# Gated mix of softmax attention and a linear-attention branch: a build-time list scheduler orders all engines, and branch B is rewritten token-major

## The chip, the cores and the metric

One core of one Trainium2 chip. The metric is the device time of one execution in microseconds (us), lower is better. Executions of one kernel usually agree within about 1%; a run more than 1.5% above the fastest of the same kernel is called slow and is left out of ratios. Engines: PE is TensorE (matmuls), PEld its weight loads, DVE is VectorE, ACT is ScalarE, POOL is GpSimd, SP issues DMAs.

## The reference, cut to what matters

2048 tokens, width 512, 32 heads of 16. Inputs and output are bf16.

```python
g = sigmoid((x * gate_w).sum(-1))                     # one gate per token
a = softmax(q k^T / 4) v  @ A_wo                      # branch A: 32 full 2048 x 2048 attentions
pq, pk = q' w_phi, k' w_phi                           # branch B: its own q', k', v'
phi_q = [softmax(pq), softmax(-pq)]; phi_k likewise   # 32 features per head
b = (phi_q (phi_k^T v')) / (phi_q sum(phi_k) + 1e-6)  @ B_wo
out = g * a + (1 - g) * b
```

Branch A needs 32 x 2048 x 2048 exponentials. They are the largest single piece of work, and in both kernels only ACT makes them.

## The kernel before

Scores of branch A are made transposed, as "units" of 128 keys x 512 queries of one head, four heads (a "pack") side by side on 32 rows each of the PE array. Five PSUM banks form a ring; ACT takes three units, then two, then three. The scores of group k need the banks that group k-2 has left, so PE can be two groups ahead of ACT and no more.

```python
def _emit_st_group(self, k):                 # scores ("QK")
    for u in range(ua, ub + 1):
        if k >= 2: deps.append((self.c_exp.sem, k - 1))        # exponential k-2 is done
        self.op("pe", lambda e: e.matmul(self.ps_ring[:, u % 5, :],
            self.kT_d[32*i:32*i+32, ...], self.qT_ring[32*i:32*i+32, ...], tile_position=(32*i, 0)), ...)
def _emit_exp_op(self, k):                   # 819 of them, 128 x 1536 or 128 x 1024
    self.op("act", lambda e: e.activation(self.ET[...], self.ps_ring[...], ACT.Exp, scale=0.25), ...)
# _emit_pv_pack: ps_ot[32*i:32*i+17] += Vaug . ET; the 17th column of V is ones, for the denominator
```

Everything else, the "side work", is put into slots between the packs by hand-made rules. It shares two PSUM banks (`mp`), and a projection is one block of four 256-column matmuls:

```python
for p in range(NPACK):
    self._run_conts(p)                       # readers put off, parts 2 and 3 of a feature tile
    for k in ops_first_at_pack[p]: self._emit_st_group(k)
    if p >= LAG: self._emit_pv_pack(p - LAG)
    for k in ops_at_pack[p]: self._emit_exp_op(k)
    self._run_side(p)                        # projections, branch B, outputs
def _proj_block(...):
    for c in range(4):
        self.op("pe", lambda e: e.matmul(mp[:, 0:256], lhs_fn(c), rhs_fn(c), start=(c == 0), stop=(c == 3)), ...)
    # then a DVE copy, put off by one slot
```

Branch B projects q' and k', multiplies by w_phi, subtracts maximum and minimum on DVE, takes 128 exponentials of 128 x 256, normalises, and works in two halves of the heads. All of x and of the weights is loaded before the first projection. Outputs for three quarters of the tokens are made at the very end, 128 columns at a time.

The softmax here doesn't subtract the row's maximum and nothing guards it: scores larger than these inputs give would overflow.

## Time and profile before

Median 1185.89 us of 4 runs (1182.9 to 1190.98). The profiled execution takes 1185.6 us. I split it by ACT: before the first score exponential starts (head), from there to the end of the last one (middle), and after it (tail).

| us | kernel before |
|---|---|
| head | 27.1 |
| middle: ACT busy | 989.7 |
| middle: ACT idle | 151.9 |
| tail | 16.9 |

From the page of the kernel before: the span, the busy times, the clock that PE was granted in 40 slices (tenths of full), and the largest group of instructions (busy us, mean ns of one, then idle before them and who ended it).

```profile
span 1185.6 us, 14920 instructions
PE 937.5 (79%) x5848; PEld 277.9 (23%) x5856; DVE 553.6 (47%) x1424; ACT 990.9 (84%) x949; POOL 22.4 (2%) x28
...
PEclk9965555667577566655575757757567556565567
...
L504 ACT ACTIVATE ET<-ps_ring 128x1536 bf16<-128x1536 f32 (+1 forms) x819 | 952.6, 1252 | 172.5 <-PE ps_ring L449 168.6
```

ACT bounds the kernel, and it waits for scores. The clock is between half and three quarters nearly everywhere. Three lines of the waits view (total us, times, longest), the first for ACT, the others for PE itself:

```profile
ACT ET L504 <- PE ps_ring L449: 168.6, 155, 25.1
...
PE ps_ot L474 <- DVE T_63 L512: 21.1, 15, 3.1
...
PE ps_mp L778 <- DVE kvz_acc L791: 9.4, 10, 1.5
```

The last two: PE stands at a matmul whose input, or whose bank, DVE has not finished. Adding up all idle time of PE in the middle that DVE ended gives 74.2 us (53.1 in front of side work, 21.1 in front of PV).

The timeline, here around a k projection:

```profile
119.05 1.04 PE L621 MATMUL ps_mp<-xT,WA 128*128 128x256 bf16 x4
120.02 0.12 PEld L449 LDWEIGHTS ps_ring<-qT_ring,kT_d 32*128 32x128 bf16 x5 [0.41 <-ACT ET L504]
120.02 1.03 PE L449 MATMUL ps_ring<-qT_ring,kT_d 32*128 32x512 bf16 x5
...
120.73 5.97 ACT L504 ACTIVATE ET<-ps_ring 128x1536 bf16<-128x1536 f32 x5 [0.87 <-PE ps_ring L449]
```

The exponential waited 0.87 us for scores that stood behind the projection in PE's queue. The end of the kernel is worse; this is the output projection at 128 columns, two banks and a DVE instruction between:

```profile
1151.11 0.66 PE L911 MATMUL ps_mp<-WoA_d,onT_A 128*128 128x128 bf16 x8 [0.22 <-DVE outt L916]
1151.54 0.61 DVE L916 SCALAR_TENSOR_TENSOR outt<-ps_mp,gcol,outB 128x128 bf16<-128x128 f32 x2 [0.23 <-PE ps_mp L911]
1152.34 0.61 PE L911 MATMUL ps_mp<-WoA_d,onT_A 128*128 128x128 bf16 x8 [0.57 <-DMA out_dram<-outt]
...
1155.35 1.02 ACT L504 ACTIVATE ET<-ps_ring 128x1024 bf16<-128x1024 f32 x1 [3.12 <-PE ps_ring L449]
```

### The profile page before, as it was taken

What the parts mean: (1) busy time and instruction counts of PE and PEld (TensorE: products, weight loads), DVE (VectorE), ACT (ScalarE), POOL (GpSimd) and SP (SyncE); (2) the same over time, 40 slices, a digit from 0 to 9 for tenths busy, and PEclk for the clock granted to TensorE, in tenths of its full rate; (3) what the DMA queues carried; (4) which work ended last, traced back from release to release, by engine and by line L of the source; (5) the groups of instructions that cost most, each with busy time, mean ns of one, the idle gap of its engine ahead of it and who ended that gap; (6) DMA issues with size and microseconds to landing.
All of it is one profiled execution on the core that took longest, in us unless ns stands there. A gap on an engine that the chain in (4) does not pass through costs nothing.

```text
span 1185.6 us, 14920 instructions
## 1 busy us (share of the span) xinstructions
PE 937.5 (79%) x5848; PEld 277.9 (23%) x5856; DVE 553.6 (47%) x1424; ACT 990.9 (84%) x949; POOL 22.4 (2%) x28
## 2 busy tenths in 40 slices
PE   4978888888778878888877877877878687787784
PEld 2422212222222222222121222212222112222132
DVE  4411111153663664645455255455563656446435
ACT  1898898989899998988898989988898788688651
POOL 4000000000000000000000000000000000000011
PEclk9965555667577566655575757757567556565567
DMA  5100000100000000000000000000000000000001
GB/s 124 37 1 1 1 1 1 54 1 2 1 1 1 1 1 1 1 1 1 1 1 1 1 1 1 1 1 1 1 1 1 1 1 1 1 2 1 0 32 41
DMA packets 13110, 9.36 MB, mean 8 GB/s; under 512 B 10736, under 2 KB 11760, under 8 KB 13040
## 3 DMA queue, kind: packets, MB, share of 16 engines
q1 hardware_dynamic: 12000, 4.74, 1.7%
q0 software_dynamic: 1040, 3.67, 0.9%
q8 instruction: 46, 0.75, 0.3%
q14 instruction: 24, 0.20, 0.1%
HBM read 4.21 MB, written 2.10 MB: 5 GB/s over the span
## 4 chain that ended last, share of the span: by engine, by line
PE 42%; ACT 29%; DVE 16%; issue 9%; another core or an unknown queue 1%; DMA 1%; SPq 1%; DVEq 0%; ACTq 0%; POOL 0%
ACT ET L504 28%; PE ps_ring L449 16%; PE ps_ot L474 11%; PE ps_mp L621 9%; DVE T_63 L512 2%; PE ps_mp L880 2%; DVE bmx L727 1%; DVE bsub L729 1%; DVE brc L748 1%; DVE bsub L732 1%; DVE bmx L725 1%; DVE brc L745 1%; ACT bexp L739 1%; SPq L540 1%
## 5 line engine op out<-in xcount | busy, mean ns | idle before, releaser
L504 ACT ACTIVATE ET<-ps_ring 128x1536 bf16<-128x1536 f32 (+1 forms) x819 | 952.6, 1252 | 172.5 <-PE ps_ring L449 168.6
L449 PE MATMUL ps_ring<-qT_ring,kT_d 32*128 32x512 bf16 x2048 | 427.0, 542 | 137.7 <-ACT ET L504 130.9
L474 PE MATMUL ps_ot<-ET,Vaug 128*17 128x512 bf16 x2048 | 281.5, 539 | 21.4 <-DVE T_63 L512 21.1
L449 PEld LDWEIGHTS ps_ring<-qT_ring,kT_d 32*128 32x128 bf16 x2048 | 78.8, 97 | 384.6 <-ACT ET L504 306.4
L474 PEld LDWEIGHTS ps_ot<-ET,Vaug 128*17 128x17 bf16 x2048 | 50.7, 90 | 246.9 <-issue 209.2
L689 DVE CAST qkT_B<-ps_mp 128x256 bf16<-128x256 f32 x64 | 27.1, 423 | 94.0 <-PE ps_mp L621 94.0
L653 DVE CAST kT_d<-ps_mp 128x256 bf16<-128x256 f32 x32 | 13.6, 425 | 97.8 <-PE ps_mp L621 97.7
L621 PE MATMUL ps_mp<-xT,WqT_v 128*128 128x256 bf16 x256 | 56.9, 367 | 1.8 <-DVE kvz_acc L791 1.4
L621 PE MATMUL ps_mp<-xT,WB 128*128 128x256 bf16 x256 | 54.4, 354 | 0.0
L670 DVE CAST qT_ring<-ps_mp 128x256 bf16<-128x256 f32 x64 | 26.9, 420 | 46.7 <-PE ps_mp L621 46.5
L512 DVE STREAM_TRANSPOSE T_63<-ps_ot 128x512 f32<-128x512 f32 x32 | 22.8, 714 | 47.3 <-PE ps_ot L474 47.0
L512 DVE STREAM_TRANSPOSE T_63<-ps_mp 128x512 f32<-128x512 f32 x32 | 22.9, 717 | 42.1 <-remote 29.9
L621 PE MATMUL ps_mp<-xT,WA 128*128 128x256 bf16 x128 | 28.7, 382 | 17.1 <-DMA xT<-in_A_x_dram 16.9
L725 DVE TENSOR_REDUCE bmx<-ps_mp 128x16 f32<-128x256 f32 x64 | 26.9, 420 | 28.4 <-PE ps_mp L718 28.4
L888 DVE CAST outB<-ps_mp 128x256 bf16<-128x256 f32 x32 | 13.6, 425 | 53.0 <-PE ps_mp L880 53.0
L944 PE MATMUL ps_mp<-WoA_d,onT_A 128*128 128x128 bf16 x64 | 17.0, 291 | 25.7 <-DVE oacc L955 6.6
L880 PE MATMUL ps_mp<-WoB_d,onT_Bc 128*128 128x256 bf16 x128 | 36.1, 381 | 0.2 <-DVE qT_ring L670 0.2
L892 DVE TENSOR_TENSOR outB<-ps_mp,outB 128x256 bf16<-128x256 f32 x32 | 13.6, 425 | 45.3 <-PE ps_mp L880 45.3
L745 DVE TENSOR_REDUCE brc<-bexp 128x16 f32<-128x256 bf16 x64 | 26.6, 416 | 15.5 <-ACT bexp L739 14.4
L621 PEld LDWEIGHTS ps_mp<-xT,WqT_v 128*128 128x128 bf16 x256 | 25.7, 120 | 29.7 <-PE ps_ring L449 10.7
L621 PEld LDWEIGHTS ps_mp<-xT,WB 128*128 128x128 bf16 x256 | 25.2, 118 | 25.7 <-issue 18.0
L812 PE MATMUL ps_mp<-iden,phiq_tile 128*128 128x128 bf16 x128 | 19.1, 303 | 14.9 <-DVE phi_qTc L821 8.4
(73 smaller groups left out, 662.9 us busy)
## 6 DMA issues: line engine op xcount, KB each, us to landing
out_dram<-outt POOLq DMA_DIRECT2D x16, 128.0 KB, 2.0
WA<-in_A_wqkv_dram POOLq DMA_DIRECT2D x1, 1536.0 KB, 8.2
WB<-in_B_wqkv_dram SPq DMA_DIRECT2D x1, 1536.0 KB, 7.6
wphi<-in_B_w_phi_dram SPq DMA_DIRECT2D x32, 0.5 KB, 1.6
WoA_d<-in_A_wo_dram SPq DMA_DIRECT2D x1, 512.0 KB, 4.5
WoB_d<-in_B_wo_dram SPq DMA_DIRECT2D x32, 16.0 KB, 1.6
xT<-in_A_x_dram SPq DMA_TRANSPOSE x4, 5.8
gw<-in_gate_w_dram SPq DMA_DIRECT2D x4, 0.2 KB, 2.5
```

Of the source, the lines that this page charges most:

```text
L449: tgt = self.op("pe", lambda e, b=b, g=g, kt=kt, ri=ri, i=i: e.matmul(self.ps_ring[:, b, :], self.kT_d[32 * i:32 * i + 32, g // 2, kt * TO ...
L474: last = self.op("pe", lambda e, i=i, h=h, kt=kt, sl=sl: e.matmul(self.ps_ot[32 * i:32 * i + VSL, :], self.Vaug[:, kt, h, :], self.ET[:, s ...
L504: tgt = self.op("act", lambda e, b0=b0, b1=b1, s0=s0, s1=s1: e.activation(self.ET[:, s0:s1 + 1, :], self.ps_ring[:, b0:b1 + 1, :], ACT.Exp ...
L512: d1 = self.op("dve", lambda e: e.transpose(self.T1[:].rearrange("p b s -> p (b s)"), src_bank_ap), deps=deps, counter=self.c_dve)
L621: last = self.op("pe", lambda e, c=c, mp=mp: e.matmul(mp[:, 0:out_cols], lhs_fn(c), rhs_fn(c), start=(c == 0), stop=(c == 3)), deps=(list( ...
L670: evac_fn=lambda e, mp: e.tensor_copy(self.qT_ring[:, ri, 256 * hc:256 * hc + 256], mp[:, 0:256]),
L689: evac_fn=lambda e, mp: e.tensor_copy(self.qkT_B[:, s, cl, 256 * hc:256 * hc + 256], mp[:, 0:256]),
L725: r1 = self.op("dve", lambda e: e.tensor_reduce(self.bmx[:, 0, :], pb3, AX.X, ALU.max), deps=[last, prev_exp], counter=self.c_dve)
L745: q1 = self.op("dve", lambda e: e.tensor_reduce(self.brc[:, 0:16], bexp0.rearrange("p (h f) -> p h f", f=DH), AX.X, ALU.add), deps=[a1, B. ...
L812: last = self.op("pe", lambda e, gg=gg, mpb=mpb, src=src: e.transpose(mpb[:, P * gg:P * gg + P], src[:, P * gg:P * gg + P], self.iden[:, : ...
L880: last = self.op("pe", lambda e, pr=pr, P4=P4, mp=mp: e.matmul(mp[:, 0:256], self.onT_Bc[:, ob, pr, tt * TOK:(tt + 1) * TOK], self.WoB_d[: ...
L944: m = self.op("pe", lambda e, mp=mp: e.matmul(mp[:, 0:128], self.onT_A[:, qc, pr, tt * TOK:(tt + 1) * TOK], self.WoA_d[:, pr, cols], start ...
```

## The change

The intent: let a scheduler at build time place every instruction of every engine, so that ACT never waits; start ACT earlier; and make branch B cheaper. The scheduler simulates the five engines with assumed durations. Each instruction has a priority and an earliest time; score groups always go first. It also hands out the two PSUM banks. Its result is a fixed order for each engine with semaphore waits. (A "head group" below is four heads with one quarter of the queries; there are 32.) Cut to its core:

```diff
+class Sched:
+    LAT = 0.09                                   # assumed time for a semaphore, us
+    def run(self):
+        ...                                      # pick the engine that can start first, and on it
+                                                 # the ready instruction of highest priority;
+                                                 # take a free bank, or wait until one is freed
+o_qk = s.op("pe", 0.42, [qk(x) for x in range(ua, ub + 1)], deps, prio=-1e5 + k)
+s.op("act", w * 0.427 + 0.09, ... ACT.Exp, ..., prio=tu)
+self.o_pv[p] = s.op("pe", 0.40, [pv(p, i) for i in range(4)], deps, prio=...)
+def c_mm(n): return max(0.075, n * 0.75e-3)      # assumed for a side matmul of n columns
+def proj(self, lhs, rhs, n, ...):                # four matmuls, each placed by itself
+    for c in range(4):
+        m = s.op("pe", self.c_mm(n), lambda e, c=c: e.matmul(self.bk(b)[:, 0:n], lhs(c), rhs(c),
+            start=(c == 0), stop=(c == 3)), ...)
-    self._run_side(p)                            # the hand-made slots go
```

The rest of it, abridged line by line. "Token-major" in the title means that branch B is now normalised with the tokens, not the features, on the 128 partitions:

```diff
+self.d_x.append(dma("sp", [xpart(j, c) for c in range(4)], ...))       # x in quarters, weights in slices
-rhs_fn=lambda c: self.xT[:, c, c0:c0 + 256], out_cols=256             # projections 512 columns wide
+rhs = self.xT[:, c, qc * QCH:(qc + 1) * QCH]
-lhs_fn=lambda c: self.WqT_v[:, c, g, :]                               # q projected twice, zero padded
+self.qT = bank * self.par[:, par]                                     # once, masked at the evacuation
-matmul(..., self.qkT_B[...], self.wphi[...])                          # q' then times w_phi, minus max, min
+self.Wp = WB^T . blockdiag(w_phi)                                     # composed once; features = x . Wp
+activation(self.phi[...], bank(128 x 512), ACT.Exp, scale=+1 or -1)   # 64, straight from PSUM
-self._norm_chain(mp, self.T2B, ...)                                   # DVE transposes for B
+transposes on PE; den * (1 + 1e-6 term) * exp(gate) folded in         # (1-g)/g, so one factor g at the end
+s.op("pe", self.c_mm(512), ... WoB x4, WoA x4 into one bank)          # outputs 512 wide, spread out
```

One slip in the new kernel: the gate's matmuls look up their bank through a variable that later code rebinds. In the order as shipped it happens to be the right bank.

## The prediction

> **What bounds the kernel now.** ScalarE's exponentials, but it is kept waiting. The page gives ACT 990.9 us busy of 1185.6; the groups give 952.6 us of that to the 819 score exponentials. By the windows its idle time is: 27 us before the first exponential; about 8 us in 27:100, 16 in 100:250, 12 in 250:400, 38 in 400:800, 27 in 800:1000, 30 in 1000:1137, 21 in 1137:1169 (the output projections queue on two PSUM banks and on the output DMA); 17 us after the last one. The table of waits names one cause: the exponential waits for the score matmuls, 155 times, 168.6 us (one of them the 25 us start). In the timeline each such wait follows a block of four 256-column projection matmuls put in front of the scores: 1.0 us at the low clock, costing 0.5 to 0.9 us.
>
> **What changes.**
> 1. Exponential work on ACT: scores unchanged. Feature exponentials go from 128 of 256 elements (427 ns) to 64 of 512. The Trainium skill, "ScalarE: Activation LUTs", section "What ACT_TABLE_LOAD costs", gives 186 ns + 0.833 ns per element with about 93 ns overlap; the trace agrees (1465 ns for 1536, 1038 for 1024). So an estimate of 0.52 us each, 33 us; ACT total about 985 us, hardly less than now.
> 2. Head: x arrives in quarters and only one slice of the weights is needed. Now four transposing DMAs issue for 13.4 us and PE starts at 16.9; a quarter should be there at about 7, first exponential at 12 to 14 (gain 14 us).
> 3. Tail: the last tiles keep only one block out of eight; 17 us becomes about 10 (gain 7). The output jam before it goes (gain about 20).
> 4. PE: padded q projections halve (65.5k to 32.8k columns), the q,k-times-Phi step goes; side columns 352k to 308k, in units of one 512-column matmul between score groups, not four.
> 5. DVE: 554 us falls to an estimated 275 to 300 (no max/min/subtract, no B norm chain). Off the critical path; it only frees banks sooner.
>
> **What limits it then.** Floor: 13 + 985 + 10 = about 1008 us. But PE is nearly as full. The trace's clock is 0.5 or 1.0, nothing between (mean 0.632), as the skill's "TensorE: Matmul & The Clock Gate", Part 1, says. At 0.5 a group of score matmuls, a PV pack, and each change of matmul kind start 0.54 us apart (0.43 without a change). Per 5 units ACT needs 2.40 us (985/410); PE at the low clock needs an estimated 2 x 0.54 + 1.25 x 0.54 + about 0.8 for side work = 2.5 to 2.6 us, at the high clock about 1.6. So ACT waits in low-clock stretches and hardly in high ones; I estimate 35 us of middle idle, against 152 now.
>
> **Predicted: 1042 us**, 8 in 10 between 1012 and 1085. Faster by over 2%: 0.97; within 2%: 0.02; slower: 0.01.
>
> **What would show it.** First score exponential at 12 to 14 us; ACT busy 980 to 990 us, 93 to 96% of the span; waits of the exponential on score matmuls 45 to 60 us in all, short ones (under 0.5 us); DVE under 310 us; mean clock 0.55 to 0.7; last exponential about 10 us before the end; no stretch like 1137:1169.
>
> **What would make it wrong.** The evenly spread side work keeps the clock at 0.5 throughout: then PE bounds, 1070 to 1090 us. Or the build-time durations (0.42 us per score group, 0.75 ns a column) differ from the chip's so that the fixed order makes ACT wait for feature projections. Or the clock stays high: near 1010.

## More of the kernel before

Section 4 of the page follows the chain of work that ended last, from the end of the kernel back to its start:

```profile
PE 42%; ACT 29%; DVE 16%; issue 9%; another core or an unknown queue 1%; DMA 1%; SPq 1%; DVEq 0%; ACTq 0%; POOL 0%
```

DVE's own work stands on that chain for 16% of the span. ("issue" is time in which an engine waited for nothing that the profile shows.) Its direct part in ACT's waits is smaller. After the start, ACT waits 154 times for scores, 143.5 us. For each of these waits I take what PE did from the end of the exponential that frees the banks to the first score matmul, and share the wait out in proportion (an estimate from the trace): about 82 us go to side matmuls that PE was executing, 31 to PE standing for DVE, 20 to PV, and 10 to the rest. How much of the 82 came late because of an earlier stall, this count does not tell.

## The result, and the profile after

Median 1072.49 us of 4 runs (1065.91 to 1084.18, one of them slow), against 1185.89. The ratio of the fast runs is 0.9014 (95% interval 0.8961 to 0.9066). Such a ratio, here and below, is the mean time of one kernel's fast runs over that of the kernel before in the same rounds, so it is not quite the ratio of the medians. The profiled execution took 1064.1 us.

| us | before | after | difference |
|---|---|---|---|
| head | 27.1 | 12.8 | -14.3 |
| middle: ACT busy | 989.7 | 976.0 | -13.7 |
| middle: ACT idle | 151.9 | 65.6 | -86.3 |
| tail | 16.9 | 9.7 | -7.2 |
| span | 1185.6 | 1064.1 | -121.5 |

The page of the new kernel, the same lines:

```profile
span 1064.1 us, 11915 instructions
PE 923.9 (87%) x5216; PEld 213.4 (20%) x5216; DVE 276.2 (26%) x478; ACT 977.3 (92%) x886; POOL 3.0 (0%) x8
...
PEclk9998966956566655555555565655556855555565
...
L511 ACT ACTIVATE ET<-ps_ring 128x1536 bf16<-128x1536 f32 (+1 forms) x819 | 948.2, 1294 | 72.6 <-PE ps_ring L497 57.9
...
L651 ACT ACTIVATE phi<-ps_mp 128x512 bf16<-128x512 f32 x64 | 35.5, 622 | 1.1 <-PE ps_mp L419 0.7
```

PE is busy for nearly as long as before, at the same mean clock (0.626, before 0.632). What has shrunk is DVE's work, to half, and the waits. The waits view of the new kernel:

```profile
ACT ET L511 <- PE ps_ring L497: 57.9, 112, 9.2
...
ACT ET L511 <- PE ps_ot L529: 11.6, 9, 3.5
...
PE ps_mp L670 <- DVE phi L657: 3.2, 7, 1.0
...
PE ps_ot L529 <- DVE T_73 L541: 1.7, 5, 0.6
```

The longest of the 112 waits, 9.2 us, is the start; in the middle 48.7 us are left. The second line is a wait that the prediction did not have: for PV, which frees the exponentials' output slots. All idle time of PE that DVE ended is now 10.7 us in the middle (9.0 and 1.7), where it was 74.2. DVE's share of the chain in section 4 of the page falls from 16% to 4%:

```profile
ACT 49%; PE 46%; DVE 4%; issue 1%; DMA 0%; SPq 0%
```

The tail, from the timeline: the last exponentials run through, and only one block per token tile is left after them.

```profile
1039.35 15.11 ACT L511 ACTIVATE ET<-ps_ring 128x1536 bf16<-128x1536 f32 x13
...
1056.66 0.71 DVE L553 STREAM_TRANSPOSE onT_A<-T_75 128x512 bf16<-128x512 bf16 x1
1057.43 1.04 PE L725 MATMUL ps_mp<-WoA,onT_A 128*128 128x512 bf16 x2 [2.32 <-DVE onT_A L553]
```

What is left of ACT's idle time depends on the clock, which in the trace is either 1.0 or 0.5:

| between first and last score exponential | us at clock 1.0 | ACT idle in them | us at clock 0.5 | ACT idle in them |
|---|---|---|---|---|
| before | 281.8 | 22.3 (7.9%) | 859.8 | 129.6 (15.1%) |
| after | 254.8 | 5.8 (2.3%) | 786.8 | 59.8 (7.6%) |

Two theories had to be tested. One about the gain: where did the 86 us of idle time go? My own answer was finer interleaving (single matmuls between score groups); rivals are less and longer work, and an order that knows when DVE will be done. One about the rest: are the remaining 66 us due to the low clock, or to too much PE work, or to wrongly assumed durations?

### The profile page after: what moved, and what is told of

Read it like the earlier page. It is cut to its first block, busy times and chain, and to the rows that moved or that the text cites. A ratio compares the mean times of both kernels' runs of the same rounds, so it can differ in the third digit from the quotient of the medians.

```text
span 1064.1 us, 11915 instructions
## 1 busy us (share of the span) xinstructions
PE 923.9 (87%) x5216; PEld 213.4 (20%) x5216; DVE 276.2 (26%) x478; ACT 977.3 (92%) x886; POOL 3.0 (0%) x8
## 4 chain that ended last, share of the span: by engine, by line
ACT 49%; PE 46%; DVE 4%; issue 1%; DMA 0%; SPq 0%
ACT ET L511 48%; PE ps_ring L497 18%; PE ps_ot L529 10%; PE ps_mp L419 8%; PE ps_mp L725 5%; PE ps_mp L670 2%; ACT phi L651 2%; PE ps_mp L682 1%; PE ps_mp L702 1%; DVE phi L657 1%; DVE fsum L655 1%; PE ps_mp L617 0%; DVE T_73 L541 0%; SPq L365 0%; DVE frec L656 0%
## 5 line engine op out<-in xcount | busy, mean ns | idle before, releaser
L511 ACT ACTIVATE ET<-ps_ring 128x1536 bf16<-128x1536 f32 (+1 forms) x819 | 948.2, 1294 | 72.6 <-PE ps_ring L497 57.9
L497 PE MATMUL ps_ring<-qT,kT 32*128 32x512 bf16 x2048 | 447.5, 543 | 113.1 <-ACT ET L511 108.9
L497 PEld LDWEIGHTS ps_ring<-qT,kT 32*128 32x128 bf16 x2048 | 82.9, 97 | 447.8 <-ACT ET L511 358.6
L655 DVE TENSOR_REDUCE fsum<-phi 128x64 f32<-128x1024 bf16 x32 | 39.0, 1218 | 266.6 <-ACT phi L651 266.6
L419 PE MATMUL ps_mp<-Wp,xT 128*128 128x512 bf16 x128 | 64.7, 577 | 0.0
L419 PE MATMUL ps_mp<-xT,WA 128*128 128x512 bf16 x128 | 51.2, 477 | 8.1 <-DMA xT<-in_A_x_dram 7.6
L657 DVE TENSOR_TENSOR phi<-phi,frec 128x1024 bf16<-128x1024 bf16 x32 | 39.1, 1222 | 0.8
L651 ACT ACTIVATE phi<-ps_mp 128x512 bf16<-128x512 f32 x64 | 35.5, 622 | 1.1 <-PE ps_mp L419 0.7
L725 PE MATMUL ps_mp<-WoA,onT_A 128*128 128x512 bf16 x64 | 32.2, 574 | 4.5 <-DVE onT_A L553 3.0
L725 PE MATMUL ps_mp<-WoB,onT_B 128*128 128x512 bf16 x64 | 33.6, 599 | 0.0
L419 PE MATMUL ps_mp<-WBV,xT 128*128 128x512 bf16 x64 | 25.1, 507 | 0.3 <-ACT phi L651 0.3
L670 PE MATMUL ps_mp<-iden,phi 128*128 128x128 bf16 x128 | 20.7, 299 | 3.2 <-DVE phi L657 3.2
L454 DVE CAST Vaug<-ps_mp 128x128 bf16<-128x128 f32 (+1 forms) x32 | 13.4, 425 | 30.6 <-PE ps_mp L419 30.4
```

The costliest lines, as they stand in the source:

```text
L419: m = s.op("pe", self.c_mm(n), lambda e, c=c: e.matmul(self.bk(b)[:, 0:n], lhs(c), rhs(c), start=(c == 0), stop=(c == 3)), deps if c == 0 ...
L497: return lambda e: e.matmul(self.ps_ring[:, x % RING, :], self.kT[32 * i:32 * i + 32, g // 2, kt * P:(kt + 1) * P], self.qT[32 * i:32 * i ...
L511: self.o_exp.append(s.op("act", w * 0.427 + 0.09, lambda e, b0=b0, s0=s0, w=w: e.activation(self.ET[:, s0:s0 + w, :], self.ps_ring[:, b0:b ...
L651: ex.append(s.op("act", 0.53, lambda e, sg=sg: e.activation(self.phi[:, ph.idx, :, sg, :], self.bk(b).rearrange("p (h f) -> p h f", f=DH), ...
L655: rd = s.op("dve", 1.15, lambda e: e.tensor_reduce(self.fsum[:, fs.idx, :], flat(), AX.X, ALU.add), ex, r + 10)
L657: sc = s.op("dve", 1.15, lambda e: e.tensor_tensor(flat(), flat(), self.frec[:, fs.idx, :, None].to_broadcast([P, 64, DH]), ALU.mult), [rc ...
```

## The experiments

Twelve variants ran, all with correct results. Ratios are against the kernel before in the same rounds; the new kernel has 0.9014.

| run | median us | ratio | mean clock, profiled | ACT idle in the middle, us |
|---|---|---|---|---|
| after | 1072.49 | 0.9014 | 0.626 | 65.6 |
| e9_blind | 1145.31 | 0.9629 | 0.569 (slow) | 163.8 (slow) |
| e2_block | 1051.07 | 0.8847 | 0.663 | 57.3 |
| e13_narrow | 1066.22 | 0.8971 | 0.614 | 68.2 |
| e12_q_twice | 1065.10 | 0.8962 | 0.663 | 66.1 |
| e4_wait_all | 1080.51 | 0.9092 | 0.628 | 65.9 |
| e8_late_out | 1058.07 | 0.8889 | 0.635 | 50.3 |
| e3_recal | 1069.36 | 0.9005 | 0.584 | 72.7 |
| e5_warmdur | 1060.29 | 0.8934 | 0.645 | 60.5 |
| e1_double | 1075.35 | 0.9066 | 0.725 | 82.8 |
| e6_ring512 | 1061.54 | 0.8922 | 0.878 (slow) | 74.3 (slow) |
| e7_adapt | 1024.22 | 0.8545 | 0.963 | 20.4 |
| e11_before_heat | 1276.81 | 1.0734 | 0.773 | 223.3 |

Where the profiled execution was a slow run it says so; totals and ratios use the fast runs. The "slow" runs here are single executions of one core, more than 1.5% above that kernel's fastest.

### Where the gain came from

**e2_block**: the four matmuls of a projection as one unit again.

```diff
-        for c in range(4):
-            m = s.op("pe", self.c_mm(n), lambda e, c=c: e.matmul(...), ...)
+        m = s.op("pe", 4 * self.c_mm(n), [lambda e, c=c: e.matmul(...) for c in range(4)], deps, ...)
```

> The four matmuls of a projection are one unit again, as in the kernel before; everything else as in the new one. If it is the single matmuls between score groups that gave the gain in the middle: waits of about 0.7 us at about 96 projections, 40 to 80 us more, 1105 to 1150. If the gain came from the smaller amount of PE and DVE work alone: no change, 1060 to 1080.

Measured: 1051 us, 2% *less* than the new kernel (0.8847, interval 0.8810 to 0.8884). So my theory falls: in the new order it is not the single matmuls that give the gain. A block still makes a score group late at the low clock, as this timeline of e2_block shows:

```profile
601.81 1.89 PE L417 MATMUL ps_mp<-xT,WA 128*128 128x512 bf16 x4
...
603.63 0.86 PE L495 MATMUL ps_ring<-qT,kT 32*128 32x512 bf16 x5
...
604.29 4.62 ACT L509 ACTIVATE ET<-ps_ring 128x1536 bf16<-128x1536 f32 x4 [1.07 <-PE ps_ring L495]
...
605.79 0.39 PE L495 MATMUL ps_ring<-qT,kT 32*128 32x512 bf16 x3 [0.76 <-ACT ET L509]
```

But it holds up no more than the same work in pieces: the idle share of ACT at the low clock is 7.6% in both kernels. And soon after this block, at 605.79 us, a group of score matmuls takes 0.39 us where one takes 0.61 at the low clock: the clock has gone up, a point that comes back below.

**e13_narrow** and **e12_q_twice**: undo "longer" and "less".

```diff
 # e13_narrow
+        for lo in range(0, n, 256):          # two times four matmuls of 256 columns
 # e12_q_twice
+        for par in range(2):
+            b, m = self.proj(...)            # the q projection made again for the second head
```

> The 512-column projections as two times four matmuls of 256 columns, one evacuation as in the new kernel: the same columns, 448 more matmuls. Rival F (longer matmuls give the gain): 20 us or more longer. Theory E: within 15 us of the new kernel's 1072, either way.

> The q projection is made twice, once for each head of a pair, as in the kernel before: 32.8 k columns of PE work more. If PE work is what counts, at the low clock 64 matmuls x 0.43 us = 27 us more PE time, total 10 to 30 us longer. If more full-array work also lifts the clock, within 10 us, clock above 0.626.

Measured: 1066 and 1065 us, both inside the new kernel's interval of ratios. In e12_q_twice 32.8 k columns more cost nothing, and the clock is higher, 0.663. Neither the width nor this part of the saved PE work is where the 86 us came from. (The other savings of branch B were not undone one by one.)

**e9_blind**: the same program and scheduler, but the scheduler believes that DVE takes no time.

```diff
+        if eng == "dve":
+            dur = 0.02
         o = Op(eng, dur, list(fns), deps, prio, rel, alloc, frees, dma, order)
```

> The new kernel, but its scheduler believes that every VectorE instruction takes 0.02 us: the order of PE is made as if results of VectorE were there at once. In the middle of the traces PE stood in front of a side or PV matmul, waiting for VectorE, for 74 us in the kernel before and 11 us in the new one, and nothing behind it in the queue could pass. Theory E (the gain in the middle comes from an order that knows when VectorE will be done): such waits rise to 30 us or more and the total by 20 to 60 us, 1090 to 1130. Rival F (it comes from less and longer work): 1060 to 1080.

Measured: 1145 us, 73 more than the new kernel and more than I had expected. PE's idle time in front of side work and PV that DVE ended rises from 10.7 to 75.1 us, the amount of the kernel before (this trace is a slow run, 1169.9 us; the four fast ones took 1142 to 1147). The timeline of e9_blind shows the mechanism:

```profile
601.71 1.23 DVE L659 TENSOR_TENSOR phi<-phi,frec 128x1024 bf16<-128x1024 bf16 x1
602.99 0.93 PE L672 MATMUL ps_mp<-iden,phi 128*128 128x128 bf16 x7 [2.94 <-DVE phi L659]
603.85 0.61 PE L499 MATMUL ps_ring<-qT,kT 32*128 32x512 bf16 x2
...
604.50 1.02 ACT L513 ACTIVATE ET<-ps_ring 128x1024 bf16<-128x1024 f32 x1 [2.40 <-PE ps_ring L499]
```

PE stands 2.94 us in front of a transpose whose input DVE is still making. The scores behind it in the queue could have run, and may not. The exponential then waits 2.40 us. The Trainium skill says it in "TensorE: Matmul & The Clock Gate", Part 2, under the step-by-step account: matmuls "stay in program order". This trace agrees. So in the new kernel an order that knows DVE's durations is needed for most of the gain in the middle: take it away, and 73 us come back (ratio 0.9629 against 0.9014), although DVE's work stays halved. DVE's share of the chain goes back up as well:

```profile
ACT 44%; PE 44%; DVE 9%; issue 2%; DMA 0%; SPq 0%; another core or an unknown queue 0%
```

That the old kernel lost its time in just this way is not shown: its order was made by hand and not by a blind scheduler. The same count as for the old trace gives a similar mixture, though: of 144.7 us that ACT waits for scores in this slow trace, about 74 go to side matmuls and 48 to PE standing for DVE. In the new kernel it is 42 and 0.5 of 48.7.

**e4_wait_all** and **e8_late_out**: undo the early start and the spread outputs.

```diff
 # e4_wait_all: every projection
-                         QCH, [self.d_wk[cp], self.d_x[j]], ...
+                         QCH, self.d_x + self.d_wv + self.d_wk + self.d_wq, ...
 # e8_late_out
-                r = self.tn(8 * (qc + 1)) + 4 + 4 * (t % 4)
+                r = self.tn(30) + t
```

> Every projection waits for all of x and of the weights, as before; the order is planned with that. First exponential at 27 to 30 us in place of 12.8, total longer by 12 to 18 us: 1080 to 1092. If the head is caught up later (other idle time shrinks), less than 8.

> The output projections of the first twelve token tiles are all put off to the last two head groups, as in the kernel before. They take about 96 x 0.43 us of PE at the low clock, 41 us, in a stretch of 60 us: total longer by 10 to 25 us. If the jam before the end had not cost the old kernel anything: under 5.

e4_wait_all: the first exponential starts at 33.0 us, 20.2 later, and later than the old kernel's 27.1. Issuing the sixteen small transposing DMAs takes 20.7 us here, where the four large ones of the old kernel took 13.4, and PE starts at 28.05, when the weights behind them have landed. In the profiled run the middle (65.9 us idle) and the tail are as in the new kernel, so nothing is caught up there. The profiled spans differ by 20.1 us, the means of the fast runs by 10.7 (1081.0 and 1070.3). The profiled run of e4_wait_all is the slowest of its four (the others had a clock of 0.640 to 0.646), that of the new kernel its fastest; the spread of the runs does not allow a better figure than 10 to 20.

e8_late_out missed: 1058 us, *less* than the new kernel. The tail does grow, to 19.6 us, but the middle loses 15 us of idle time. Late outputs as such therefore need not jam the end. The old timeline above suggests what did: eight small matmuls, then a wait for DVE or for the output DMA, with the scores behind them. No run tests that.

### What is left, and the clock

**e3_recal** and **e5_warmdur**: only the assumed durations of PE, to what the traces show at the low and at the high clock.

```diff
-        return max(0.075, n * 0.75e-3)        # scores 0.42, PV 0.40
+        return max(0.12, n * 0.83e-3 + 0.11)  # e3_recal: scores 0.54, PV 0.54
+        return max(0.09, n * 0.43e-3 + 0.08)  # e5_warmdur: scores 0.33, PV 0.33
```

> Only the assumed durations, set to what the trace shows at the low clock (0.54 us a score group or PV pack, 0.83 ns a column plus 0.11 us). Rival C: the order now fits the chip and the middle idle time falls by half, 1035 to 1045. Theory A: PE has as much to do at the same clock, so 1055 to 1090.

> Control for the two runs above: only the durations that the build-time scheduler assumes are changed, to those of the high clock (0.33 us a score group, 0.33 a PV pack, 0.43 ns a column plus 0.08 us). Theory A: little change, 1055 to 1090, since the clock stays low. Rival C (the fixed order is wrong because the assumed durations are): a change of over 20 us one way or the other.

Measured 1069 and 1060 us, each within its expectation for theory A. Setting PE's durations to those of the low or of the high clock (0.54 or 0.33 us a score group) changes the ratio by 1% or less, and those of the low clock, at which PE mostly runs, do not remove the waits. (In e3_recal much of the wait moves from scores to PV: 41.1 us of its exponentials' idle time is ended by PV, which frees their output slots.)

**e1_double** and **e6_ring512**: more PE work that does nothing, to lift the clock. Both use the assumed durations of e5_warmdur.

```diff
 # e1_double: each projection, from the fifth head group on, and half of each output block
-        for c in range(4):
+        for c in ([0, 1, 2, 3] if prio > self.tn(4) else []) + [4, 5, 6, 7]:   # start=(c <= 4)
 # e6_ring512: before the scores of a group, into the bank that they will overwrite
+    e.matmul(self.ps_ring[:, x % RING, 0:512], self.kT[:, cp, keys], self.qT[:, n % 4, :], start=True, stop=True)
```

> From the seventh quarter-million on (after the first four head groups) each projection of four 512-column matmuls is preceded by the same four matmuls again, into the same bank, which the real ones then overwrite: about 200 k more columns of full-array work that do nothing. In the two traces the clock stayed or went high where a 3.4 us stretch held about 1500 or more columns of full-array matmuls (median 2000) and went low below about 1000. Theory A (low clock, from too thin full-array work, makes PE late): mean clock rises from 0.626 to 0.75 or more, idle time of ScalarE in the middle falls from 66 us to under 40, total 1020 to 1050. Rival B (PE simply has too much work, whatever its clock): 200 k columns more cost at least 80 us at the high clock and 170 at the low one; total 1120 or more.

> One useless full-array matmul of 512 columns in front of every group of score matmuls, into the bank that the scores then overwrite: 419 k columns more, evenly spread, about 1450 per 3.4 us. Theory A: clock above 0.9, middle idle under 35 us, total 1010 to 1045. Rival B: 419 k columns more make PE the bound, total above 1200.

(The opening of the first text is a slip; it means "from the fifth head group on".) e1_double gave 1075 us, outside what either theory had: clock 0.725, idle 12.5 us of 473 at the high clock (2.6%), but 70.3 of 583 at the low one (12.1%). The doubled work helps where it lifts the clock and hurts where it does not; against its control e5_warmdur (1060 us) it loses 15 us. e6_ring512 adds 419 k columns, more than all side work, and is no slower than the new kernel or than e5_warmdur: 1062 us. That rules out rival B, the amount of PE work at any clock. It also missed theory A's 1045: in the profiled run, a slow one, 252 us stayed at the low clock, with 22% idle; the clock of the fast runs was 0.897 to 0.912.

In the traces every interval of one clock but the last, which the end cuts off, is a multiple of 3.413 us long, so I cut them into stretches of that length. Counting the full-array matmul columns (128 rows x 128 columns of the array) that start in each stretch shows why. All 14 traces together (some records are missing: e9_blind's trace shows 276 k of the 308 k side columns), the share of stretches that are followed by a high-clock one:

| full-array columns in the stretch | 0-511 | 512-1023 | 1024-1535 | 1536-2047 | 2048-2559 | 2560-3071 |
|---|---|---|---|---|---|---|
| clock now 1.0 | 0.02 | 0.14 | 0.69 | 0.89 | 0.99 | 0.99 |
| clock now 0.5 | 0.00 | 0.00 | 0.05 | 0.17 | 0.58 | 0.82 |

It takes about 1500 columns to stay high nine times in ten, and over 2000 to come back more often than not. Scores and PV, which use the array in strips (32 rows; 17 columns), are present all the time and do not keep the clock up by themselves (0.02 and 0.00 in the first column); no run took them away, so what they add is not known. The new kernel spreads 308 k side columns over some 1040 us, about 1010 per stretch (an estimate: 308/1040 x 3.41): evenly too thin.

**e7_adapt**: put useless columns only where the plan is thin.

```diff
+            if o.room:                                  # a score group, as it is placed in the plan
+                near = sum(x.cols + x.heat for x in recent if x.start > now - 2.4)
+                o.heat = max(0, min(o.room, (2000 - near + 255) // 256 * 256))   # room: 512 or 1024
+                o.dur += o.heat * 0.43e-3 + (0.06 if o.heat else 0)
```

> Useless full-array matmuls only where the planned order is thin: before a group of score matmuls the scheduler adds 0 to 1024 columns so that the last 2.4 us of its plan hold about 2000 full-array columns (about 390 k in all, against 308 k of useful side columns). From the four runs so far the clock stays high where 3.4 us hold 1536 columns or more, and comes back from low only with 2048 to 2560. Theory A (low clock is what is left of ScalarE's waits): clock above 0.9, middle idle 20 to 35 us, 1010 to 1035, faster than the new kernel and than e6_ring512. Rival D (what is left comes from the coupling of the engines, two score groups ahead, at any clock): middle idle stays near 60, 1050 to 1065.

Measured: the three fast runs take 1008.75 to 1023.24 us, the three slow ones 1025.19 to 1029.12 (clock 0.929 to 0.935); median of the six 1024.22, ratio 0.8545 (0.8477 to 0.8614), 5% under the new kernel (0.8545/0.9014), and 4% under e5_warmdur, which has the same assumed durations without the added columns. The profiled run is one of the two near 1009; the other four had a clock of 0.929 to 0.940. Middle idle 20.4 us, of which only 4.1 in 917 us at the high clock. Rival D, coupling of the engines at any clock, falls. The page of e7_adapt, and below it the window 480:500 of the new kernel and of e7_adapt (busy us of PE, PEld, DVE, ACT, POOL, then the clock):

```profile
span 1007.7 us, 13541 instructions
PE 891.0 (88%) x6028; PEld 262.1 (26%) x6028; DVE 275.0 (27%) x478; ACT 966.4 (96%) x886; POOL 3.0 (0%) x8
...
PEclk9999999999999899978995999999999999999998
```

```profile
480.00:500.00 20.00, 19.05 (x101) 4.65 (x100) 8.65 (x16) 17.77 (x17) 0.00 (x0) 0.50 0.00 1
```

```profile
480.00:500.00 20.00, 18.53 (x128) 5.44 (x128) 5.35 (x13) 20.00 (x19) 0.00 (x0) 1.00 0.02 8
```

PE is busy for nearly the same share in both, and executes 27 matmuls more in the second. ACT has no gap in it.

**e11_before_heat**: the matmul of e6_ring512 in the old kernel.

```diff
+            if u == ua:
+                self.op("pe", lambda e: e.matmul(self.ps_ring[:, b, :], self.kT_d[:, g // 2, keys],
+                    self.qT_ring[:, ri, :], start=True, stop=True), deps=deps)
```

> The kernel before with one useless full-array matmul of 512 columns in front of every score group, as in e6_ring512. The clock was low for 860 of 1142 us between its first and last exponential, with 15% of them idle, and 8% idle at the high one. Clock above 0.85; middle idle from 152 to about 110 us; total 1130 to 1165. If the old order costs the same at any clock: 1180 or more.

Measured: 1277 us, 7% slower; my expectation failed. The clock rose to 0.773, the idle share at the high clock stayed (8.5%, before 7.9%), and at the low clock it doubled (29%). The 8% at full clock stay with the old kernel; whether its order or its larger DVE work causes them, this run does not separate. In the new kernel and its variants with sound DVE durations it is 0.4 to 2.6%, save e3_recal, and in e9_blind it is 5.4%. In e3_recal it is 10% (17.0 of 167 us), and I did not follow that up. Useless columns do not pay everywhere: in the old order they cost more than they brought.

## Why the prediction was right or wrong, point by point

The time, 1072.49 us, lies inside 1012 to 1085, and 30 us above the centre.

- **Right: head, tail, DVE.** First exponential at 12.8 us (12 to 14), tail 9.7 (about 10), DVE 276 us (275 to 300), no jam before the end.
- **ACT's work** fell to 977.3 us, below the 980 to 990 expected. Its share of the span is 92%, not 93 to 96. From the skill's "ScalarE: Activation LUTs", section "What ACT_TABLE_LOAD costs", one 512-element exponential comes to an estimated 613 ns (186 + 0.833 x 512); the trace has 622. I had costed it at 520 with the overlap, 33 us in all, and the group is busy for 35.5.
- **The mis-sized term: "35 us of middle idle".** It measured 65.6 us. In the profiled run, 22 us above the centre, these 31 us too many were partly offset by ACT's work, 9 us below the 985 of the sum, which was luck; the median lies 8 us higher still, and so the 30 us only look like this one term. I had expected waits "in low-clock stretches and hardly in high ones": 59.8 and 5.8 us show that this was right, and e7_adapt showed it by intervention. But the low clock lasted for 787 us of 1042, with 7.6% idle. I had named as a risk that evenly spread side work keeps the clock low; it is what happened, in the larger part, and I gave it too little weight.
- **"45 to 60 us in all, short ones (under 0.5 us)"** is right for the total, 57.9 us with the start, and half right for the length: of the 111 waits after the start, 79 are under 0.5 us, but the 32 longer ones hold 21.3 of their 48.7 us.
- **Wrong: the remedy for the old waits, and DVE's part in them.** I put the gain down to "units of one 512-column matmul between score groups, not four". e2_block has blocks and is faster. That side matmuls stood in front of the scores was read rightly (about 82 of 143.5 us). But "one cause" was what I read from ACT's side, and I did not ask what PE was doing meanwhile: in 74 us of the middle it stood still for DVE. e9_blind brought that back and with it most of the loss. I had called DVE's shorter work "off the critical path"; the page of the kernel before has DVE on that path for 16% of the span, and now for 4%.

What stays open: how much of the loss in e9_blind comes from the waits themselves and how much from its lower clock (0.60 to 0.61 in the fast runs, 0.626 in the new kernel's profiled one); whether the smaller DVE work alone, in the old order, would have brought some of the gain, which no run tests; why e8_late_out has less idle time in the middle, beyond the work that it moves out of it; and why e7_adapt has two sorts of runs, 1009 and 1023 to 1029 us.

## What to carry to other kernels

When one engine waits for another that is itself "busy", look at what the second one waits for: in an in-order queue, one instruction placed too early holds up ready work behind it. Here a build-time order needed roughly right durations for the engine in between (believing DVE free cost 73 us), while setting PE's own to the low or the high clock changed the time by 1% or less. Before calling PE full, look at its clock: here 3.4 us stretches with too few full-array columns were mostly followed by half clock, and useless matmuls in thin stretches were worth 4 to 5% in the new kernel, while one before every score group made the old one 7% slower.

## What the Trainium skill lacked or had wrong

- "TensorE: Matmul & The Clock Gate", Part 1 and the table under "Why this matters for your kernels": it asks for no idle gaps of over about 3 us between bursts of matmuls. In the new kernel PE was busy for 87% of the span, and after its start no idle gap of PE was longer than 2.3 us (1.1 us in the middle), yet the clock was 0.5 for 787 of 1042 us. What went with the clock was the number of full-array columns in 3.41 us (about 1500 to stay high, over 2000 to come back, from 14 traces); score and PV matmuls in strips of the array did not keep it up by themselves. Raising that number raised the mean clock from 0.626 to 0.963 at the same PE busy share (87 and 88%). The page has no such threshold and no difference between staying and coming back. That the clock is either half or full is as the page says.
- "TensorEngine Tiling (Array Packing)", Key Properties: it says that a change of tiling mode drains the engine, and gives no time. At the low clock, in the kernel before at 122.23 to 123.31 us, a score group and the PV pack after it start 0.54 us apart, as do the PV pack and the next scores; two score groups in a row and the PV behind them take 0.96 us (120.02 to 120.98), so a step without a change is about 0.42. A change costs about 0.12 us there.
- No page warns that side work spread evenly can run at a lower clock than the same work in bursts: with blocks of four matmuls in e2_block the mean clock was 0.663, with single ones 0.626, and the kernel was 2% faster (1051 us, 1072 us).
